# Order of loads, sums and splits around the superblock borders of a three-stage kernel

## The chip, the cores and the metric

The kernel runs as one program on one core of a Trainium2 chip. The metric is the device time of one execution in microseconds; the kernel before takes 1987.39 us (median of 3 runs, 1986.38 to 1988.28).

## The reference

Three stages are chained. A linear attention (4 batches, 8 heads, 576 positions, 64 channels) gives 2304 tokens of 512 channels. A dense two-layer MLP with a leaky ReLU follows. The last stage is a mixture of 8 experts in which every token goes through every expert, weighted by a matrix P that 8 rounds of row and column scaling balance:

```python
P = np.exp(logits - logits.max())          # logits = x @ w_gate, 2304 x 8
for _ in range(8):
    P /= P.sum(1, keepdims=True) + 1e-09
    P /= P.sum(0, keepdims=True) + 1e-09
    P *= N / E
for e in range(E):                          # E = 8, w1 512 x 1024, w2 1024 x 512
    h = np.maximum(x @ w1[e], 0.0)
    out += P[:, e:e + 1] * (h @ w2[e])
```

Everything is float32.

## The kernel before

All matrix products run as three TensorE products of split operands: a value is kept as a rounded high part and a low part, and `split` makes them, the high part by a copy on ScalarE (L526) and the low part by a subtraction on VectorE (L527). The expert stage also uses a scheme with seven block products in place of eight, so sums and differences of the blocks of x, w1, w2 and the hidden values are needed first; their names are A11, S1 to S4 and so on for weights and B11, B21, B22, T1 to T4 for the data side.

The expert stage covers the tokens in 3 superblocks of 768 tokens (two blocks of 384). The first layer of all experts is cut into NQ = 32 pairs of units, so there are NG = 96 groups, `group(i)`: groups 0 to 31 are the first superblock, 32 to 63 the second, 64 to 95 the third. Group i makes the seven first-layer products of its pair. In the first superblock the second layer is done plainly (`y_tile`), while the split operands of both layers are made from the raw weights and written out to HBM (`keep_w1`, `keep_w2`, `keep`). From group 34 on the second layer is done by `y_pass` with the seven products too, and all weight operands come back from HBM through a ring of 256 KB chunks (`ring_load`).

A group has seven steps t0 to t6, and the program text is written in that order, one half step at a time. t0 to t3 issue the seven first-layer products, with the copies of their sums (c1 at L977, c2 at L1000 and L1002) and the activations `relu_split` or `relu_p`; t4 to t6 issue second-layer work. Splits whose low part is still to be made are put on a list (`rest`), and the `drain` of a later step issues it. TensorE, ScalarE, GpSimd and SyncE (SP, which issues every DMA) take their instructions in that written order; each engine waits at its next instruction until the operands are there.

What surrounds the borders between superblocks:

- `second_load(i)` (L523) loads the 512 KB of raw w2 of pair i. In an odd group i of the first superblock `second_ops` issues it for pair i-1 at the end of t0 and for pair i at the end of t1; `pair_w2` splits them at t6 of that group and at t0 of the next one.
- In group 31, t0 issues `ring_load(0, 7)`, then `keep_w1(31)`; t1 issues `p_load(1, 0)` (two loads of rows of P, L774). `ring_load(7, 14)` stands in step t4 of group 31, `ring_load(14, 18)` in t0 of group 32, `ring_load(18, 22)` in t2 of group 33. The chunks 0 to 6 are used by group 32, 7 to 13 by group 33, 14 to 27 by group 34.
- `x_ahead` and `x_next` make the sums of x of the next superblock (GpSimd) and their splits into the tiles that the first-layer products read. For the second superblock both start in group 31; for the third, `x_ahead` runs in group 58 and `x_next` in group 63. The sum T4 is made in `x_next`; for the third superblock the low parts of B11 and T2 are made on GpSimd.
- `op_split` splits the hidden values of a pair of groups into the seven operands of `y_pass`, from the raw products in `raw_q(0)` to `raw_q(3)`; `sub_raw` (L797) makes the differences, on VectorE or GpSimd. `ends(i)` is true for group 63; groups 95 (NG-1), 96 and 97 form the end. `y_pass` adds its results by VectorE (L824) or by a copy (L818) and a GpSimd addition (L819).
- `y_out` transposes finished outputs and copies them out of PSUM, by ScalarE (L897) and VectorE (L895) in turn.
- c2 and the sum T4 come from one pool of two buffers (tag "hh"); before, every group takes the next buffer for c2.

Of the kernel before, what the change touches and what calls it, by code (L numbers as in the profile page):

```python
# [22 lines left out]
def kernel(  # L23
# [500 lines left out]

    def split(hi, lo, a, eng=nc.vector):
        nc.scalar.copy(hi, a)  # L526
        return lambda: eng.tensor_tensor(lo, a, r32(hi), op=ALU.subtract)  # L527

# [76 lines left out]
    def x_split(sb, name, a):  # L605
        eng = nc.gpsimd if sb > 1 and name in ("B11", "T2") else nc.vector
        f = split(xt(name)[:, 0], xt(name)[:, 1], a, eng)

        def end():
            f()  # L610
            ready.add(("xt", sb, name))

        return end
# [28 lines left out]
    def x_ahead(sb):  # L642
        b11, b12, b21, b22 = x_quads(sb)
        t1, t2 = (
            raw_q(k) if sb == 1
            else acc[1][:, k * XS // 2 : (k + 1) * XS // 2].rearrange("p (c n) -> p c n", c=KC // 2)
            for k in range(2)
        )
        x_parts[sb] = t1, t2
        nc.gpsimd.tensor_tensor(t1, b12, b11, op=ALU.subtract)  # L650
        nc.gpsimd.tensor_tensor(t2, b22, t1, op=ALU.subtract)
        nc.gpsimd.tensor_tensor(b12, b22, b12, op=ALU.subtract)

    def x_next(sb):
        b11, b12, b21, b22 = x_quads(sb)
        t1, t2 = x_parts[sb]
        yield
        t4 = hp_.tile([P, KC // 2, BLK], F32, tag="hh", name=f"t4_{sb}")
        rest.append(x_split(sb, "B11", b11))
        yield  # L660
        nc.gpsimd.tensor_tensor(t4, b21, t2, op=ALU.subtract)
        if sb > 1:
            rest.append(x_split(sb, "T2", t2))
        yield
        if sb == 1:
            rest.append(x_split(sb, "T2", t2))
        rest.append(x_split(sb, "T1", t1))
        yield
        rest.append(x_split(sb, "B21", b21))
        yield  # L670
        rest.append(x_split(sb, "T3", b12))
        rest.append(x_split(sb, "B22", b22))
        yield
        rest.append(x_split(sb, "T4", t4))

# [203 lines left out]
    def y_out(sb, dt, ya):  # L879

        c11, c22, dd, cc = ya
        nc.vector.tensor_tensor(dd, c22, dd, op=ALU.subtract)
        nc.vector.tensor_tensor(cc, c22, cc, op=ALU.subtract)
        for th, quads in enumerate(((c11, cc), (dd, c22))):
            for t in range(TB):
                tt = th * TB + t
                if tt % 2 == 0:
                    yield PE_NEXT
                pt = (bank if sb == NSB - 1 else side_bank)(f"po{sb}_{dt}_{tt}")[:, : 2 * P]
                for h, a in enumerate(quads):  # L890
                    nc.tensor.transpose(pt[:, h * P : (h + 1) * P], a[:, t * P : (t + 1) * P], ident)
                n = dt * 2 * TB + tt
                o = acc[1][:, n % 6 * 2 * P : (n % 6 + 1) * 2 * P]
                if t % 2:
                    nc.vector.tensor_copy(o, pt)  # L895
                else:
                    nc.scalar.copy(o, pt)  # L897
                tok = 2 * sb * TB + tt
                nc.sync.dma_start(
                    out[tok * P : (tok + 1) * P, :].rearrange("p (h t n) -> p h t n", h=2, t=2)[:, :, dt],  # L900
                    o.rearrange("p (h n) -> p h n", h=2),
                )

    rest, late = [], []

    def ends(i):
        return NQ < i < NG - 1 and i % NQ == NQ - 1

    def group(i):
# [7 lines left out]
        if i < NG:  # L917
            bk = [bank(f"p{n}_{i}")[:, :BLK] for n in "abcd"]
            c2 = hp_.tile([P, 2, BLK], F32, tag="hh", name=f"c2_{i}")
            c1 = hp_.tile([P, BLK], F32, tag="g", name=f"c1_{i}", bufs=1)  # L920
            add = lambda o, x, y: nc.vector.tensor_tensor(o, x, y, op=ALU.add)  # L921
# [17 lines left out]
        def second_ops(t):  # L939
# [11 lines left out]
            if half == 1 and i < NQ:  # L951
                if t < 2:
                    second_load(i - 1 + t)
                if t == 6:
                    rest.append(pair_w2(i - 1))
                    late.append(lambda: keep_w2(i - 1))

        def t0():
            drain((rest, late))
            if i == NQ - 1:  # L960
                ring_load(0, 7)
            if i == NQ:
                ring_load(14, 18)
            if i == NQ + 2:
                ring_load(22, 30)
            if i >= NG:
                y_steps(0)
                if i == NG:
                    rest.append(op_split(LG, "T2", raw_q(0)))
                    rest.append(op_split(LG, "T3", raw_q(1)))  # L970
                return
            if i < NQ:
                keep_w1(i)
# [5 lines left out]
            add(c1, bk[1], c1)  # L979
            second_ops(0)  # L980
            if new and half and i < NG - 1:
                rest.append(op_split(eg, "T1", raw_q(0)))
            if ends(i - 1):
                sub_raw(nc.vector, 2, 0, 2)
                rest.append(op_split(eg - 1, "T3", raw_q(1)))

        def t1():
            drain()
            if i == NQ - 1:
                p_load(1, 0)  # L990
            if new and i % (2 * EG) == 2 and i + 2 < NG:
                n = i // (2 * EG) + 1
                p_load(n // E, n % E)
            if i >= NG:
                y_steps(1)
                if i == NG:
                    rest.append(op_split(LG, "T4", raw_q(2)))
                return
# [7 lines left out]
            if ends(i - 1):  # L1006
                rest.append(op_split(eg - 1, "T4", raw_q(2)))

        def t2():
            drain()  # L1010
            if i == NQ + 1:
                ring_load(18, 22)
            if i >= NG:
                y_steps(2)
                return
            product(bk[0], i, "A12", "B21", False)
# [4 lines left out]
            product(bk[2], i, "S4", "B22", False)  # L1021
            add(c2[:, 0], bk[2], c1)
            if i == NG - 1:
                rest.append(op_split(eg, "T1", raw_q(0)))
# [3 lines left out]
        def t3():  # L1028
# [6 lines left out]
            if new:  # L1035
                relu_p(i, 0, raw_q(2 * half)[:, 1], c1)
                relu_p(i, 1, raw_q(2 * half + 1), c2)
                if half:
                    sub_raw(nc.vector, 0, 3, 0)
                    if not ends(i):  # L1040
                        sub_raw(nc.gpsimd, 1, 3, 1)
# [5 lines left out]
            if i == NQ - 1:  # L1047
                rest.append(lambda: ring_load(7, 14))

        def t4():  # L1050
# [7 lines left out]
            if new:  # L1058
                if half == 0:
                    rest.append(op_split(eg, "B11", raw_q(0)))  # L1060
                else:
                    rest.append(op_split(eg, "B21", raw_q(2)))
                    rest.append(op_split(eg, "B22", raw_q(3)))

        def t5():
# [5 lines left out]
            if new:  # L1071
                if half == 0:
                    sub_raw(nc.gpsimd, 0, 1, 0)
                else:
                    if ends(i):
                        sub_raw(nc.gpsimd, 1, 3, 1)
                    else:
# [119 lines left out]
    T3 = H2 * (NPH - 1)  # L1197
    at(T3 + 8, pair0)

    for n, t in enumerate((18, 19, 20, 21, 22, 23, 27, 28, 29, 30, 35)):  # L1200
# [88 lines left out]
```

## Time and profile before

| | us |
|---|---|
| median of 3 runs | 1987.39 |
| profiled execution | 1986.21 |
| its span, first to last instruction | 1984.4 |
| TensorE busy | 1938.1 (98%) |
| VectorE busy | 1491.1 (75%) |
| ScalarE busy | 805.2 (41%) |
| GpSimd busy | 708.3 (36%) |
| mean granted TensorE clock | 0.991 of full speed |

The median is 1.2 us above the profiled execution. The share of TensorE leaves 46 us of the span in which it is idle, and short stretches in which its granted clock is lower; the table by stretches in the last section shows where some of that lies. In the rows there, "[3.98 <-ACT c L977]" means that the engine was idle for 3.98 us before the row and that line 977 on ScalarE ended the idle time. PE is TensorE, DVE VectorE, ACT ScalarE, POOL GpSimd, SPq the queue of SyncE.

### The profile page before, as it was taken

The numbers are of one execution on the slowest core, as the hardware profiler recorded it, in microseconds if no ns is written. First come the engines' busy times: TensorE is split into PE (matmuls) and PEld (weight loads), VectorE is DVE, ScalarE is ACT, GpSimd is POOL, SyncE is SP. The second block draws the span as 40 slices with busy tenths as digits, with TensorE's granted clock in tenths as the row PEclk, the third lists the DMA queues.
The fourth block names the chain that finished last, engine by engine and source line by source line (L and its number), as shares of the span: only waits on it lengthen the run. The fifth ranks groups of instructions, "written<-read, shape, count | busy, mean of one in ns | idle before, by whom it ended". The sixth has DMA issues, their size and how long they took to land.

```text
span 1984.4 us, 30153 instructions
## 1 busy us (share of the span) xinstructions
PE 1938.1 (98%) x10757; PEld 1864.1 (94%) x10757; DVE 1491.1 (75%) x2214; ACT 805.2 (41%) x1480; POOL 708.3 (36%) x514
## 2 busy tenths in 40 slices
PE   7999999999999999999989999999999999999998
PEld 6999999999898988899879999999999999999997
DVE  7766535354788787887876888887887888888885
ACT  6744323233444444444433333333344433333333
POOL 4124313100133333343412444435553344434433
PEclk8999999999999999999989999999999999999999
DMA  6402111030388988888778888878878788887884
GB/s 249 166 11 75 54 32 54 22 117 1 133 281 291 313 300 301 298 306 310 268 267 305 260 259 264 257 246 273 256 243 251 250 272 261 261 261 263 258 256 134
DMA packets 237075, 430.43 MB, mean 217 GB/s; under 512 B 19952, under 2 KB 38528, under 8 KB 236928
## 3 DMA queue, kind: packets, MB, share of 16 engines
q1 hardware_dynamic: 236928, 428.51, 65.4%
q8 instruction: 87, 1.43, 0.3%
q14 instruction: 60, 0.49, 0.1%
HBM read 306.20 MB, written 122.23 MB: 216 GB/s over the span
## 4 chain that ended last, share of the span: by engine, by line
PE 46%; DMA 9%; DVE 6%; POOL 2%; ACT 2%; issue 1%; SPq 1%; DVEq 0%; POOLq 0%; ACTq 0%
PE e L199 23%; PE pc L199 6%; PE pd L199 6%; PE pa L199 6%; DMA mo_t<-in_w 6%; PE pb L199 3%; DMA d<-wb_t 2%; DMA d<-wa 1%; DVE c L921 1%; DVE wa L527 1%; POOL mo_t L534 1%; DVE mo_t L797 1%; DVE mo_t L783 1%; ACT wa L526 1%; DVE wb_t L527 1%
## 5 line engine op out<-in xcount | busy, mean ns | idle before, releaser
L819 POOL TENSOR_TENSOR acc<-acc,acc 128x384 f32<-128x384 f32 x188 | 277.0, 1473 | 301.7 <-ACT acc L818 292.0
L199 PE MATMUL e<-wb_t,xs 128*128 128x512 f32 x1152 | 270.4, 393 | 0.0
L199 PE MATMUL e<-xs,wb_t 128*128 128x384 f32 x1392 | 262.7, 335 | 5.6 <-DVE acc L824 3.0
L199 PEld LDWEIGHTS e<-wb_t,xs 128*128 128x128 f32 x1152 | 217.1, 189 | 44.3 <-DVE rc L422 0.2
L199 PEld LDWEIGHTS e<-xs,wb_t 128*128 128x128 f32 x1392 | 242.8, 188 | 6.8 <-DVE acc L824 3.7
L199 PE MATMUL e<-wa,wb_t 128*128 128x384 f32 x1296 | 244.3, 336 | 0.4 <-DVE acc L824 0.3
L527 DVE TENSOR_TENSOR wa<-mo_t,wa 128x768 fp32r<-128x768 f32 (+2 forms) x194 | 201.3, 1053 | 36.9 <-ACT wa L526 35.7
L199 PEld LDWEIGHTS e<-wa,wb_t 128*128 128x128 f32 x1296 | 227.5, 189 | 1.0 <-DVE acc L824 0.7
L818 ACT COPY acc<-e 128x384 f32<-128x384 f32 x188 | 90.3, 480 | 292.5 <-PE e L199 277.8
L797 POOL TENSOR_TENSOR mo_t<-mo_t 128x768 f32<-128x768 f32 x64 | 118.4, 1850 | 244.9 <-DVE mo_t L783 218.2
L526 ACT CAST wa<-mo_t 128x768 fp32r<-128x768 f32 (+2 forms) x194 | 157.5, 842 | 58.4 <-DVE mo_t L797 22.5
L217 DVE TENSOR_TENSOR hh<-g,hh 128x384 fp32r<-128x384 f32 x96 | 61.5, 641 | 156.6 <-ACT g L216 156.5
L533 POOL TENSOR_TENSOR mo_t<-mo_t 128x256 f32<-128x256 f32 x32 | 30.1, 940 | 390.1 <-DMA mo_t<-in_w 168.4
L824 DVE TENSOR_TENSOR acc<-e,acc 128x384 f32<-128x384 f32 x242 | 125.1, 548 | 37.8 <-PE e L199 28.9
L527 DVE TENSOR_TENSOR xs<-mo_t,xs 128x768 fp32r<-128x768 f32 x119 | 125.6, 1066 | 37.1 <-ACT xs L526 37.1
L199 PE MATMUL pd<-xs,wb_t 128*128 128x384 f32 x744 | 149.9, 335 | 2.8 <-DVE xs L527 2.8
L199 PE MATMUL pa<-xs,wb_t 128*128 128x384 f32 x744 | 150.2, 336 | 1.0 <-ACT c L977 1.0
L199 PE MATMUL pc<-xs,wb_t 128*128 128x384 f32 x744 | 149.1, 334 | 0.0
L215 ACT ACTIVATE hh<-ph 128x384 fp32r<-128x384 f32 x96 | 47.3, 493 | 242.3 <-PE y L199 227.6
L199 PEld LDWEIGHTS pd<-xs,wb_t 128*128 128x128 f32 x744 | 130.9, 188 | 3.2 <-DVE xs L527 3.1
L199 PEld LDWEIGHTS pa<-xs,wb_t 128*128 128x128 f32 x744 | 131.4, 189 | 1.8 <-ACT c L977 1.7
L783 DVE SCALAR_TENSOR_TENSOR mo_t<-c,mo_t 128x768 f32<-128x768 f32 (+1 forms) x128 | 128.9, 1011 | 3.0
(164 smaller groups left out, 3638.6 us busy)
## 6 DMA issues: line engine op xcount, KB each, us to landing
wb_t<-d SPq DMA_DIRECT2D x882, 256.0 KB, 3.2
d<-wa SPq DMA_DIRECT2D x32, 1792.0 KB, 8.6
d<-wb_t SPq DMA_DIRECT2D x90, 512.0 KB, 4.0
mo_t<-in_w SPq DMA_DIRECT2D x64, 512.0 KB, 9.6
raw<-in_wm SPq DMA_DIRECT2D x32, 512.0 KB, 3.7
d<-wa SPq DMA_DIRECT2D x22, 512.0 KB, 3.2
mo_t<-pd SPq DMA_DIRECT2D x32, 192.0 KB, 8.1
v<-in_vt SPq DMA_DIRECT2D x16, 320.0 KB, 5.9
```

Source lines behind the costliest of these rows:

```text
L199: nc.tensor.matmul(o, a, b, start=start, stop=stop, **more)
L215: nc.scalar.activation(hh[:, 0, :], p, AF.Prelu, alpha=0.01)
L217: nc.vector.tensor_tensor(hh[:, 1, :], g, r32(hh[:, 0, :]), op=ALU.subtract)
L526: nc.scalar.copy(hi, a)
L527: return lambda: eng.tensor_tensor(lo, a, r32(hi), op=ALU.subtract)
L533: nc.gpsimd.tensor_tensor(s[:, 0], a21, a22, op=ALU.add)
L534: nc.gpsimd.tensor_tensor(a21, a11, a21, op=ALU.subtract)
L783: nc.vector.scalar_tensor_tensor(o, p, 0.0, r, op0=ALU.max, op1=ALU.mult)
L797: eng.tensor_tensor(raw_q(o), raw_q(x), raw_q(y), op=ALU.subtract)
L818: nc.scalar.copy(t, bk[b])
L819: nc.gpsimd.tensor_tensor(c22, c22, t, op=ALU.add)
L824: return nc.vector.tensor_tensor(a, bk[b], a, op=ALU.add)
```

## The change

- `second_load(0)` and `second_load(1)` are issued in the last phase of the MLP, 26 half steps after its start. In odd groups from 3 on, `second_load(i-1)` is the first thing in t0, ahead of `keep_w1(i)` and `pair_sums`.
- In group 31 the order on SP becomes: `second_load(30)` in t0; `p_load`, `second_load(31)`, `ring_load(0, 7)` in t1; `keep_w1(31)` in t3. `ring_load(7, 14)` goes to t3 of group 32, and 14 to 21 are loaded together in t2 of group 33.
- `x_ahead` makes all four sums, T4 too, one in each half step; `x_next` only splits, T1 one step later than before, and all low parts are made on VectorE.
- From group 33 on, all groups use one c2 buffer, and T4 has the other.
- For group 63, B21 and B22 are split in t0 and t1 of the next group instead of t4, the difference in `raw_q(2)` moves from t0 to t1 and the split of T4 from t1 to t2 of the next group, and the difference in `raw_q(1)` moves from GpSimd to VectorE.
- At the end: the difference in `raw_q(0)` of group 94 and that in `raw_q(1)` of group 95 move from GpSimd to VectorE (the latter from t3 to t5), that in `raw_q(2)` moves from t5 of group 95 to t2 of group 96, B21 and B22 are split in t1 of group 96 instead of t4 of group 95, T4 in t2.
- `y_out` copies by ScalarE alone.

The diff, cut to its core:

```diff
-        eng = nc.gpsimd if sb > 1 and name in ("B11", "T2") else nc.vector
-        f = split(xt(name)[:, 0], xt(name)[:, 1], a, eng)
+        f = split(xt(name)[:, 0], xt(name)[:, 1], a)
...
+        t4 = hp_.tile([P, KC // 2, BLK], F32, tag="hh", name=f"t4_{sb}")
         nc.gpsimd.tensor_tensor(t1, b12, b11, op=ALU.subtract)
+        yield
         nc.gpsimd.tensor_tensor(t2, b22, t1, op=ALU.subtract)
+        yield
+        nc.gpsimd.tensor_tensor(t4, b21, t2, op=ALU.subtract)
+        yield
         nc.gpsimd.tensor_tensor(b12, b22, b12, op=ALU.subtract)
...
+        for names in ((), ("B11",), (), ("T2",), ("T1", "B21"), ("T3", "B22"), ("T4",)):
+            for n in names:
+                rest.append(x_split(sb, n, x_parts[sb][n]))
+            yield
...
-                if t % 2:
-                    nc.vector.tensor_copy(o, pt)
-                else:
-                    nc.scalar.copy(o, pt)
+                nc.scalar.copy(o, pt)
...
-            c2 = hp_.tile([P, 2, BLK], F32, tag="hh", name=f"c2_{i}")
+            if i <= NQ:
+                c2_t[0] = hp_.tile([P, 2, BLK], F32, tag="hh", name=f"c2_{i}")
+            c2 = c2_t[0]
...
-                if t < 2:
+                if t < 2 and i > 1 and i + t < NQ:
                     second_load(i - 1 + t)
...
             drain((rest, late))
-            if i == NQ - 1:
-                ring_load(0, 7)
-            if i == NQ:
-                ring_load(14, 18)
+            if half:
+                second_ops(0)
...
-            if i < NQ:
+            if i < NQ - 1:
                 keep_w1(i)
...
             if ends(i - 1):
-                sub_raw(nc.vector, 2, 0, 2)
                 rest.append(op_split(eg - 1, "T3", raw_q(1)))
+                rest.append(op_split(eg - 1, "B21", raw_q(2)))
...
             if i == NQ - 1:
                 p_load(1, 0)
+                second_load(i)
+                ring_load(0, 7)
...
                 if i == NG:
-                    rest.append(op_split(LG, "T4", raw_q(2)))
+                    rest.append(op_split(LG, "B21", raw_q(2)))
+                    rest.append(op_split(LG, "B22", raw_q(3)))
...
             if ends(i - 1):
-                rest.append(op_split(eg - 1, "T4", raw_q(2)))
+                sub_raw(nc.vector, 2, 0, 2)
+                rest.append(op_split(eg - 1, "B22", raw_q(3)))
...
             if i == NQ + 1:
-                ring_load(18, 22)
+                ring_load(14, 22)
...
+                if i == NG:
+                    sub_raw(nc.vector, 2, 0, 2)
+                    rest.append(op_split(LG, "T4", raw_q(2)))
...
+            if ends(i - 1):
+                rest.append(op_split(eg - 1, "T4", raw_q(2)))
...
-                    if not ends(i):
+                    if not ends(i) and i < NG - 1:
                         sub_raw(nc.gpsimd, 1, 3, 1)
...
             if i == NQ - 1:
-                rest.append(lambda: ring_load(7, 14))
+                keep_w1(i)
+            if i == NQ:
+                ring_load(7, 14)
...
-                else:
+                elif not ends(i) and i < NG - 1:
                     rest.append(op_split(eg, "B21", raw_q(2)))
                     rest.append(op_split(eg, "B22", raw_q(3)))
...
-                    sub_raw(nc.gpsimd, 0, 1, 0)
+                    sub_raw(nc.gpsimd if i < NG - 2 else nc.vector, 0, 1, 0)
                 else:
-                    if ends(i):
-                        sub_raw(nc.gpsimd, 1, 3, 1)
+                    if ends(i) or i == NG - 1:
+                        sub_raw(nc.vector, 1, 3, 1)
...
+    at(T3 + 26, second_load, 0)
+    at(T3 + 26, second_load, 1)
```

## Rows read from the trace of the kernel before

**Rows 1.** Busy time by stretch: PE, PEld, DVE, ACT, POOL, clock, DMA share, GB/s.
```profile
996.70:1024.60 27.90, 19.32 (x80) 16.93 (x79) 19.37 (x25) 8.37 (x13) 4.61 (x3) 0.76 0.85 306
1024.60:1463.20 438.60, 438.03 (x2515) 436.26 (x2514) 360.57 (x489) 165.26 (x288) 187.80 (x118) 1.00 0.81 260
1463.20:1489.70 26.50, 23.67 (x127) 23.35 (x127) 24.04 (x27) 13.34 (x22) 14.49 (x8) 0.94 0.75 250
1932.30:1984.40 52.10, 42.48 (x235) 40.08 (x234) 32.19 (x47) 15.07 (x29) 18.12 (x14) 0.95 0.46 140
```

**Rows 2.** TensorE in order of time, groups 32 and 33: start, duration, instruction, idle before.
```profile
1005.02 2.29 PE L199 MATMUL pa<-xs,wa 128*128 128x384 f32 x6 [3.98 <-ACT c L977]
1011.90 2.29 PE L199 MATMUL pc<-xs,wa 128*128 128x384 f32 x6 [4.60 <-ACT c L1000]
...
1031.87 8.36 PE L199 MATMUL e<-wb_t,xs 128*128 128x512 f32 x36
```

**Rows 3.** ScalarE in the same stretch: the splits of raw w2 of pairs 30, 31.
```profile
1002.81 1.04 ACT L526 CAST wb_t<-mo_t 128x1024 fp32r<-128x1024 f32 x1 [4.91 <-DMA mo_t<-in_w]
...
1010.43 1.04 ACT L526 CAST wb_t<-mo_t 128x1024 fp32r<-128x1024 f32 x1 [5.46 <-DMA mo_t<-in_w]
```

**Rows 4.** The queue of SyncE in groups 31 and 32: issue start and time.
```profile
987.00 4.53 SPq L706 DMA_DIRECT2D wa<-d  x7
991.57 0.43 SPq L550 DMA_DIRECT2D d<-wa  x1
992.11 0.50 SPq L523 DMA_DIRECT2D mo_t<-in_w  x1
992.65 3.92 SPq L774 DMA_DIRECT2D mo_t<-pd  x2
996.91 1.51 SPq L523 DMA_DIRECT2D mo_t<-in_w  x1
1001.60 7.83 SPq L706 DMA_DIRECT2D wa<-d  x7
```

**Rows 5.** DMA issues: count, KB each, median us to landing; whole span, then 960:1060.
```profile
wb_t<-d SPq DMA_DIRECT2D x882, 256.0 KB, 3.2
...
wa<-d SPq DMA_DIRECT2D x14, 256.0 KB, 5.9
```

**Rows 6.** TensorE in order of time, groups 58, 64 and 65.
```profile
1394.44 1.32 PE L199 MATMUL pa<-xs,wb_t 128*128 128x384 f32 x6 [0.57 <-ACT c L977]
...
1484.06 1.63 PE L199 MATMUL pd<-xs,wb_t 128*128 128x384 f32 x5 [2.83 <-DVE xs L527]
...
1509.91 1.32 PE L199 MATMUL e<-xs,wb_t 128*128 128x384 f32 x6 [2.01 <-DVE acc L895]
```

**Rows 7.** VectorE, then GpSimd, in order of time around the border of groups 63 and 64.
```profile
1478.32 2.61 DVE L797 TENSOR_TENSOR mo_t<-mo_t 128x768 f32<-128x768 f32 x1
...
1483.06 1.81 DVE L527 TENSOR_TENSOR xs<-acc,xs 128x768 fp32r<-128x768 f32 x2
...
1488.40 0.94 DVE L797 TENSOR_TENSOR mo_t<-mo_t 128x768 f32<-128x768 f32 x1
...
1477.94 2.18 POOL L797 TENSOR_TENSOR mo_t<-mo_t 128x768 f32<-128x768 f32 x1
```

**Rows 8.** TensorE in order of time at the end, group 96.
```profile
1950.79 1.34 PE L199 MATMUL e<-xs,wb_t 128*128 128x384 f32 x6 [2.99 <-DVE acc L824]
...
1952.46 6.87 PE L199 MATMUL e<-wa,wb_t 128*128 128x384 f32 x30 [0.33 <-DVE acc L824]
```

**Rows 9.** VectorE in order of time at the end, groups 94 to 96.
```profile
1933.79 0.96 DVE L783 SCALAR_TENSOR_TENSOR mo_t<-c,mo_t 128x768 f32<-128x768 f32 x1
...
1946.84 3.43 DVE L527 TENSOR_TENSOR xs<-mo_t,xs 128x768 fp32r<-128x768 f32 x2
...
1959.83 0.55 DVE L824 TENSOR_TENSOR acc<-e,acc 128x384 f32<-128x384 f32 x1
```

**Rows 10.** ScalarE at the end, group 95: the copy into c2.
```profile
1936.95 0.48 ACT L1000 COPY c<-pc 128x384 f32<-128x384 f32 x1
```

More of the change, by code (lines that the diff above doesn't have):

```diff
@@ L523, in second_load, with split @@
         nc.sync.dma_start(r2(i), w[u : u + 2, :, DM:].rearrange("u p n -> p u n"))
-    def split(hi, lo, a, eng=nc.vector):
+    def split(hi, lo, a):
         nc.scalar.copy(hi, a)
-        return lambda: eng.tensor_tensor(lo, a, r32(hi), op=ALU.subtract)
+        return lambda: nc.vector.tensor_tensor(lo, a, r32(hi), op=ALU.subtract)
     def pair_sums(i):
@@ L648, in x_ahead @@
         )
-        x_parts[sb] = t1, t2
+        t4 = hp_.tile([P, KC // 2, BLK], F32, tag="hh", name=f"t4_{sb}")
+        x_parts[sb] = {"B11": b11, "T2": t2, "T1": t1, "T3": b12, "B21": b21, "B22": b22, "T4": t4}
         nc.gpsimd.tensor_tensor(t1, b12, b11, op=ALU.subtract)
+        yield
         nc.gpsimd.tensor_tensor(t2, b22, t1, op=ALU.subtract)
+        yield
+        nc.gpsimd.tensor_tensor(t4, b21, t2, op=ALU.subtract)
+        yield
         nc.gpsimd.tensor_tensor(b12, b22, b12, op=ALU.subtract)
     def x_next(sb):
[L655 to L674, printed above, removed]
+        for names in ((), ("B11",), (), ("T2",), ("T1", "B21"), ("T3", "B22"), ("T4",)):
+            for n in names:
+                rest.append(x_split(sb, n, x_parts[sb][n]))
+            yield
     LG = NG // 2 - 1
@@ L904 @@
     rest, late = [], []
+    c2_t = [None]
     def ends(i):
@@ L968, in t0 @@
                 if i == NG:
+                    rest.append(op_split(LG, "T3", raw_q(1)))
                     rest.append(op_split(LG, "T2", raw_q(0)))
-                    rest.append(op_split(LG, "T3", raw_q(1)))
                 return
-            if i < NQ:
+            if i < NQ - 1:
                 keep_w1(i)
@@ L979, in t0 @@
             add(c1, bk[1], c1)
-            second_ops(0)
+            if half == 0:
+                second_ops(0)
             if new and half and i < NG - 1:
```

## The prediction
> **What bounds the kernel now.** I read first the busy table by stretches, then TensorE's waits in order of time, then the engine that ended each wait. In the long middle of the expert stage TensorE is busy for 438.03 of 438.60 us at full clock [rows 1]: nothing off TensorE is worth anything there. Its 2515 matmuls give 0.1742 us each, so a product of six takes 1.045 us and a group of 84 takes 14.6 us. What can be won lies in stretches where TensorE stands still or runs at the lower clock: the border of the first and second superblock (996.7 to 1024.6, busy 19.32 of 27.90 us, clock 0.76), the second border (1463.2 to 1489.7, 23.67 of 26.50, clock 0.94) and the end (1932.3 on, clock 0.95) [rows 1]. 0.76 is a mixture of the two levels, 1.2 and 2.4 GHz: six matmuls after the first wait took 2.29 us [rows 2].
>
> First border: TensorE waits 3.98 us for the copy into c1 and 4.60 us for the copy into c2 [rows 2]. Those copies are short; ScalarE takes them in order and stood 4.91 and 5.46 us in front of the splits of raw w2 of pairs 30 and 31, for a DMA [rows 3]. On SP seven ring loads (1792 KB) and `keep_w1` (seven double chunks, 1792 KB) went ahead of the load of pair 30, and the two loads of P also ahead of that of pair 31, issued only at 996.91 [rows 4]. At the stretch's 306 GB/s [rows 1] the 4096 KB up to the end of load 30 take 13.7 us from 987.0, to 1000.7; its reader started at 1002.81. So the loads are late because of their place in the queue.
>
> Second border: TensorE waits 2.83 us for a low part on VectorE, and later 2.01 us for VectorE's copy of an output [rows 6]. VectorE is simply behind: the same 128x768 difference takes 0.94 us with GpSimd idle and 2.61 us beside a GpSimd difference of 2.18 us [rows 7]. The end: 2.99 and 0.33 us for the additions that empty PSUM, behind two splits that took 3.43 us in place of 1.81 [rows 7 to 9], and 30 matmuls in 6.87 us.
>
> **First border, term by term.** What it loses now: 42 products at 0.1742 are 7.3 us, the 36 wide ones 8.36 less the 0.16 by which records overlap, together 15.5; the stretch took 27.9, so 12.4 us.
>
> After the change load 30 is issued where the ring loads stood, 987.0. Then P takes between 1.0 us (two issues at 0.5) and 3.92 [rows 4], then load 31, at 988.5 to 991.4. Ahead of the end of load 31 lie 512+384+512 KB, 4.7 us at 306 GB/s: both have landed by about 992 to 996, before ScalarE comes to them (about 998 and 1001, by its copies before and with T1's copy of 0.9 us added). Both waits of rows 3 go. What becomes late next:
> - Ring loads 0 to 6 are moved past P and load 31, so issued from 989 to 992. With 3.2 to 5.9 us to landing [rows 5] the first is there at 992.2 to 997.8; group 32 wants it at 996.7. Cost 0 to 1.1, I take 0.2.
> - `keep_w1(31)` behind them delays nobody but ring loads 7 to 13, which overwrite what it reads; the old order had those at 1001.6 [rows 4].
> - Ring loads 7 to 13 now stand behind `keep_w2(31)`, which waits for VectorE's low part of pair 31. I put that at 1003 to 1006, the first landing at 1006 to 1013; group 33 wants it at 1012.2. Cost 0 to 2, I take 0.3, as the issue's 0.65 us a chunk (4.53/7) runs faster than TensorE uses them.
> - ScalarE has T1's copy later than before, so c1 and c2 come up to 1 us late; I take 0.4.
> - Ring loads 14 to 21 together in group 33: eight issues of 0.65 us from about 1015, wanted from 1027 on: hidden.
>
> Gain 12.4 - 0.9 = 11.5 (8.3 to 12.4).
>
> The DMA order has a rule in the Trainium skill, "DMA: Bandwidth & Descriptors", section "Queues, rings and completion order": each DMA engine consumes the descriptors of a ring in ring order. It speaks for the raw loads and as much against ring loads 0 to 6, now behind 1408 KB. The late load 30 agrees with it; what it makes of the ring loads is the first bullet, worked out from rows.
>
> **Early raw loads of pairs 0 and 1, and `second_load` ahead of `keep_w1`.** They change what ScalarE waits for in the first superblock. I have no row of a TensorE wait there that they end, and cost them at nothing; if the earlier load should push `keep_w1` back, TensorE doesn't see that, as it is read back 32 groups later.
>
> **Second border.** Now lost: 26.5 less 126 matmuls at 0.1742 (21.95), 4.5 us. VectorE's work ahead of T3's low part changes by: B21 and B22 of group 63 out (1.8), low parts of B11 and T2 in (1.8), the difference beside GpSimd from 2.61 to 0.94 (-1.7). GpSimd's own two splits and T4's sum also leave this stretch; by the 1.67 us that one GpSimd difference costs VectorE [rows 7] these three are worth 0 to 5, I take 2.5. So T3 comes 1.7 to 6.7 us earlier, I take 4.2, against a wait of 2.83: gone, or 1.1 left at the worst. Behind the border group 64 must now make four splits (3.6 us) in the 7.3 us before its `y_pass` uses them: cost 0 to 3, I take 0.5. The output copy by ScalarE (0.3 to 0.5 us, as its other copies) ends the 2.01; I take 1.9 (1.0 to 2.0). Sum 4.5 - 0.5 + 1.9 = 5.9 (1.4 to 6.5).
>
> **Group 58** now makes four sums in place of three on GpSimd. Three made TensorE wait 0.57 us there [rows 6]. One more costs VectorE 1.7 us by rows 7; VectorE is busy 360.57 of 438.60 us [rows 1], so 2.6 us of a group are free to take it up. I take 0.3 (0 to 1.8). The Trainium skill, "SBUF — State Buffer", section "Who interferes with whom", would make it dearer: the engine that comes second to the shared ports is fully blocked for the whole instruction. By that the fourth sum holds VectorE for all of GpSimd's 2.18 us [rows 7], and TensorE for 0.5 more at most: it stays inside the bound.
>
> **End.** Now lost 2.99 + 0.33 and 6.87 - 30 x 0.1742 - 0.16 = 1.5 of lower clock: 4.8 us. With B21 and B22 gone from group 95 and both GpSimd differences made by VectorE at 0.94, the additions that empty PSUM come some 3 us earlier, and the 2.99 goes. But the two splits and a difference (2.8 us) now stand between the passes of group 96, where the addition at 1959.83 [rows 9] already came just in time. I take 1.2 of these 2.8 as a new wait: gain 3.6 (2.0 to 4.8).
>
> **Sum.** 11.5 + 5.9 - 0.3 + 3.6 = 20.7 us. The profiled execution took 1986.21 and should become 1965.5; the median of the runs is 1.2 above it, so 1987.39 - 20.7 = 1966.7. The bounds add up to 9.9 and 23.7, that is 1977.5 and 1963.7; all at an end at once is unlikely, so the forecast's own range is 1963.7 to 1972.
>
> **Rivals.**
> - The waits move. Ring loads 7 to 13 behind the keep of pair 31, the four splits behind the second border and the three pieces in group 96 all hang on VectorE, which has 18% to spare; where it is further behind than I put it, the terms fall to their low ends. For: every wait of rows 6 and 8 is VectorE's or behind it. Against: seven GpSimd pieces that slow it leave. Gain about 12: 1975. Chance 0.13.
> - The raw loads come no sooner, because `second_load(30)`, now first in the queue, waits for readers of its buffer, or the DMA engines (share 0.85) are the limit. Against: at 987.0 SP was past the keeps of the pair before. The first border stays: gain 9.2, 1978.2. Chance 0.07.
> - Slower: the single c2 buffer. ScalarE's copy into c2 must now wait until VectorE's `relu_p` of the group before has read it. The narrowest place has 1936.95 - 1934.75 = 2.2 us left [rows 9, 10], where one group follows the other after 7.3 us; in all others it is 14.6, so 9.5 us. It decides if VectorE falls 9.5 us further behind; above 20.7/62 = 0.33 us a group the kernel is slower than before, and at 0.5 us, 1997. Against: VectorE has 2.6 us a group to catch up. Chance 0.04.
> - The whole gain falls within the measurement because several of these meet: 1985. Chance 0.04.
> - More than the bounds, from waits of the first superblock that I left out: 1961. Chance 0.04.
>
> **How the numbers follow.** The forecast has 0.68. The predicted time is its 1966.7. Leaving out about 0.15, the range reaches to the two partial cases and to the last: 1961 to 1978. About 0.2% (4 us) is what a measurement can tell from no change here. Faster by more: 0.68 + 0.13 + 0.07 + 0.04, less a little for what I don't see, 0.90; within 0.05; slower 0.05.
>
> **What would show it.** Right: the stretch of group 32 takes about 16 to 17 us at a clock of 1.00, ScalarE has no DMA wait ahead of the two raw splits, no wait of more than 1 us for VectorE in groups 64 and 65, and none of 3 us in group 96. A wait of TensorE for "DMA wa<-d" in group 32 or 33 shows the ring loads late; one for VectorE's L527 or L824 in group 64 or 96 shows the deferred splits. The forecast is wrong if the clock still falls at the first border, or if ScalarE's L1000 waits for VectorE's L783 in group after group.

## The result and the profile after

The changed kernel takes 1970.17 us (median of 5 runs, 1969.0 to 1970.39), the kernel before 1988.28 us beside it (5 runs). The ratio is 0.991, with a 95% interval of 0.9895 to 0.9924: 18 us faster, where 20.7 were predicted (1966.7, range 1961 to 1978). The profiled execution of after took 1970.39 us, its span 1968.2.

First the view of [rows 1], for the same stretches: the first border with the group behind it, the middle, the second border, the end.

```profile
997.90:1013.50 15.60, 15.58 (x78) 14.17 (x79) 15.56 (x22) 5.69 (x9) 2.92 (x3) 1.00 1.04 387
1013.50:1030.60 17.10, 15.82 (x79) 13.98 (x78) 13.27 (x19) 5.53 (x9) 3.94 (x2) 1.00 0.90 330
1030.60:1455.60 425.00, 423.44 (x2438) 422.15 (x2438) 350.19 (x473) 159.84 (x280) 187.89 (x118) 1.00 0.82 262
1455.60:1482.10 26.50, 26.50 (x153) 26.30 (x153) 24.92 (x34) 15.11 (x25) 6.31 (x5) 1.00 0.86 279
1920.20:1968.20 48.00, 40.70 (x236) 38.82 (x234) 30.77 (x47) 15.32 (x31) 14.37 (x12) 0.97 0.51 152
```

Group 32, 27.9 us at a clock of 0.76 before, now takes 15.6 us at 1.00. In the stretch at the second border TensorE is busy throughout (a wait of 1.55 us falls behind it); the end is 4 us shorter. In the middle TensorE stands idle for 1.6 us (0.6 before), and in group 33 for 1.3.

Next TensorE in order of time, where it waits, at the first border, in groups 58 to 60, at the second border and at the end (start, duration, instruction, idle before). These answer [rows 2, 6, 8].

```profile
997.92 1.30 PE L199 MATMUL pa<-xs,wa 128*128 128x384 f32 x6 [1.06 <-DMA wa<-d]
...
1019.13 1.15 PE L199 MATMUL pa<-xs,wa 128*128 128x384 f32 x5 [1.27 <-ACT c L963]
...
1385.44 1.33 PE L199 MATMUL pa<-xs,wb_t 128*128 128x384 f32 x6 [0.57 <-ACT c L963]
...
1402.13 1.32 PE L199 MATMUL pc<-xs,wb_t 128*128 128x384 f32 x6 [0.78 <-ACT c L990]
...
1490.87 0.55 PE L879 MATMUL po<-ident,acc 128*128 128x128 f32 x3 [1.55 <-DVE acc L871]
...
1936.25 2.35 PE L199 MATMUL e<-xs,wb_t 128*128 128x384 f32 x12 [0.46 <-DVE acc L812]
...
1945.88 2.34 PE L199 MATMUL e<-wa,wb_t 128*128 128x384 f32 x12 [0.92 <-issue]
```

The waits of 3.98, 4.60, 2.83, 2.01 and 2.99 us are gone, and small ones stand in their places. (L963 and L990 are the copies into c1 and c2, L871 the subtractions of `y_out`, L812 the additions that empty PSUM.)

The queue of SyncE and the splits of raw w2 on ScalarE, groups 31 and 32, answering [rows 3, 4]:

```profile
982.17 0.36 SPq L560 DMA_DIRECT2D d<-wa  x1
...
984.49 0.84 SPq L523 DMA_DIRECT2D mo_t<-in_w  x1
985.38 1.88 SPq L762 DMA_DIRECT2D mo_t<-pd  x2
987.31 0.59 SPq L523 DMA_DIRECT2D mo_t<-in_w  x1
987.99 8.12 SPq L694 DMA_DIRECT2D wa<-d  x7
997.13 0.37 SPq L550 DMA_DIRECT2D d<-wa  x1
...
1007.56 3.19 SPq L694 DMA_DIRECT2D wa<-d  x7
...
996.81 1.04 ACT L526 CAST wb_t<-mo_t 128x1024 fp32r<-128x1024 f32 x1
...
999.64 1.06 ACT L526 CAST wb_t<-mo_t 128x1024 fp32r<-128x1024 f32 x1
```

Both splits now start without a wait for a DMA: the raw loads come in time.

Where the time went is told most plainly by the starts of the 96 groups (first matmul into pa), after against before. The head, up to group 0, took 3.1 us more (503.43 against 500.30); nothing in it explains that, and in the other runs below it varies from 501.4 to 505.1. From there on, the changed kernel gains 19.3 us: 1.7 in many small waits of groups 0 to 30, 10.8 in groups 31 to 33 (60.3 to 49.5), 4.4 in groups 64 to 66 (54.1 to 49.7) and 4.2 from group 95 on (52.1 to 47.9). It loses 1.4 in groups 59 and 60, and 0.4 in group 35; the latter shows in only one other run, the last, and is put down to no part of the change. As the head alone can hide 3 us, single runs are compared below by stretches; the period of a group without a wait is 15.51 us in groups 0 to 33 and 14.56 behind them.

### The profile page after: what moved, and what is told of

Same layout as the page of the kernel before. It is cut to its first block, busy times and chain, and to the rows that moved or that the text cites. A ratio compares the mean times of both kernels' runs of the same rounds, so it can differ in the third digit from the quotient of the medians.

```text
span 1968.2 us, 30157 instructions
## 1 busy us (share of the span) xinstructions
PE 1933.6 (98%) x10757; PEld 1860.9 (95%) x10757; DVE 1484.8 (75%) x2213; ACT 807.1 (41%) x1486; POOL 692.4 (35%) x509
## 4 chain that ended last, share of the span: by engine, by line
PE 58%; DVE 7%; issue 1%; DMA 1%; ACT 1%; SPq 0%; POOL 0%; DVEq 0%; ACTq 0%
PE e L199 30%; PE pc L199 8%; PE pd L199 8%; PE pa L199 8%; PE pb L199 4%; DVE c L909 1%; DVE mo_t L771 1%; DVE wa L527 1%; DVE mo_t L785 1%; DVE xs L527 1%; DMA wb_t<-d 1%; DVE acc L812 0%; DVE acc L745 0%; DMA d<-wa 0%; ACT wa L526 0%
## 5 line engine op out<-in xcount | busy, mean ns | idle before, releaser
L199 PE MATMUL e<-xs,wb_t 128*128 128x384 f32 x1488 | 280.7, 334 | 1.0 <-ACT acc L882 0.6
L199 PEld LDWEIGHTS e<-xs,wb_t 128*128 128x128 f32 x1488 | 259.7, 188 | 1.7 <-ACT acc L882 0.8
L199 PE MATMUL e<-wa,wb_t 128*128 128x384 f32 x1200 | 227.5, 334 | 0.9 <-issue 0.9
L199 PEld LDWEIGHTS e<-wa,wb_t 128*128 128x128 f32 x1200 | 209.6, 188 | 1.2 <-issue 1.2
L785 POOL TENSOR_TENSOR mo_t<-mo_t 128x768 f32<-128x768 f32 x61 | 113.3, 1858 | 230.0 <-DVE mo_t L771 212.6
L526 ACT CAST wa<-mo_t 128x768 fp32r<-128x768 f32 (+2 forms) x186 | 151.5, 842 | 72.0 <-DVE mo_t L785 34.6
L812 DVE TENSOR_TENSOR acc<-e,acc 128x384 f32<-128x384 f32 x242 | 125.1, 548 | 34.0 <-PE e L199 24.6
L199 PEld LDWEIGHTS pc<-xs,wb_t 128*128 128x128 f32 x744 | 130.7, 188 | 1.3 <-ACT c L990 1.3
```

Source lines behind the costliest of these rows:

```text
L199: nc.tensor.matmul(o, a, b, start=start, stop=stop, **more)
L785: eng.tensor_tensor(raw_q(o), raw_q(x), raw_q(y), op=ALU.subtract)
L812: return nc.vector.tensor_tensor(a, bk[b], a, op=ALU.add)
```

## The experiments

**One: the old order of SyncE, in the changed kernel.** Groups 31 to 33 get back their old order of issues; all else stays.

```diff
-            if half:
+            if half and i != NQ - 1:
                 second_ops(0)
+            if i == NQ - 1:
+                ring_load(0, 7)
+            if i == NQ:
+                ring_load(14, 18)
...
-            if i < NQ - 1:
+            if i < NQ:
                 keep_w1(i)
...
                 p_load(1, 0)
-                second_load(i)
-                ring_load(0, 7)
...
-                keep_w1(i)
-            if i == NQ:
-                ring_load(7, 14)
+                rest.append(lambda: ring_load(7, 14))
```

> The changed kernel with the order on SP of groups 31 to 33 put back (ring loads 0 to 6 and the keep of pair 31 ahead of the raw loads of pairs 30 and 31). If the place of the raw loads in the queue makes the stall of the first border, the group 32 takes again about 27.9 us in place of 15.6, ScalarE waits for the DMA ahead of both raw splits, and the run is some 11 us slower than the changed kernel (about 1981). If it was the earlier sums of x or the single c2 buffer that ended the stall, group 32 stays below 17 us and the time below 1973.

1975.78 us against 1988.15 (ratio 0.9937, 0.9922 to 0.9952). Groups 31 to 33 take 55.2 us: the raw loads are late again, but less so than before.

```profile
1004.52 1.31 PE L199 MATMUL pa<-xs,wa 128*128 128x384 f32 x6 [1.41 <-ACT c L967]
1010.55 2.29 PE L199 MATMUL pc<-xs,wa 128*128 128x384 f32 x6 [4.71 <-ACT c L992]
```

So the old order returns only about half of the gain. Something else in the change pays the other half.

**Two: the new order alone, in the kernel before.** The mirror image.

```diff
             if i == NQ - 1:
-                ring_load(0, 7)
-            if i == NQ:
-                ring_load(14, 18)
+                second_ops(0)
...
-            if i < NQ:
+            if i < NQ - 1:
                 keep_w1(i)
...
                 p_load(1, 0)
+                second_load(i)
+                ring_load(0, 7)
...
-                rest.append(lambda: ring_load(7, 14))
+                keep_w1(i)
+            if i == NQ:
+                ring_load(7, 14)
```

> The kernel before with nothing but the new order on SP in groups 31 to 33. By the queue theory groups 31 to 33 together fall from 60.3 to about 49.5 us and the run gains about 11 us (1977). If the gain needs the other parts too (less work for VectorE at the border), a new stall of several us for VectorE shows in group 32 and the gain is below 6.

1980.07 us (ratio 0.9964, 0.9951 to 0.9976), groups 31 to 33 53.2 us: the order alone is worth 7.1 us of 60.3. What is left are waits for an operand and for the ring loads, which start late because the whole queue does:

```profile
984.19 0.97 PE L199 MATMUL pb<-xs,wa 128*128 128x384 f32 x4 [1.50 <-DVE wa L527]
...
1001.68 2.03 PE L199 MATMUL pa<-xs,wa 128*128 128x384 f32 x6 [3.10 <-DMA wa<-d]
```

Where the queue starts late is seen at the keep that opens it in group 31 (`d<-wa`, S4's). It waits for VectorE's low part of wa. VectorE and GpSimd in order of time there, in the kernel before:

```profile
980.17 4.48 DVE L527 TENSOR_TENSOR wa<-mo_t,wa 128x768 fp32r<-128x768 f32 x2
...
979.73 1.86 POOL L651 TENSOR_TENSOR mo_t<-acc,mo_t 128x768 f32<-128x768 f32 x1 [1.70 <-DVE wa L527]
981.55 2.55 POOL L652 TENSOR_TENSOR acc<-acc 128x768 f32<-128x768 f32 x1
```

and in the changed kernel:

```profile
979.30 2.85 DVE L527 TENSOR_TENSOR wa<-mo_t,wa 128x768 fp32r<-128x768 f32 x2
...
987.63 2.19 DVE L909 TENSOR_TENSOR c<-c 128x384 f32<-128x384 f32 x1
...
978.86 1.87 POOL L652 TENSOR_TENSOR mo_t<-acc,mo_t 128x768 f32<-128x768 f32 x1 [1.69 <-DVE wa L527]
985.05 1.84 POOL L654 TENSOR_TENSOR t<-acc,mo_t 128x768 f32<-128x768 f32 x1 [4.32 <-DVE xs L752]
986.85 2.56 POOL L656 TENSOR_TENSOR acc<-acc 128x768 f32<-128x768 f32 x1
```

Before, GpSimd went from T2's sum straight on to b12's, and VectorE's two low parts beside it took 4.48 us. Now T4's sum comes between; it waits 4.32 us for its buffer, b12's sum falls some 4 us later against the group, and the low parts take 2.85. Its price moved to the c addition at 987.63 (2.19 us, 0.55 otherwise), for which TensorE does not wait. That was a reading of two traces; the next run tests it.

**Three: GpSimd's old order alone**, at the first border of the changed kernel.

```diff
         nc.gpsimd.tensor_tensor(t2, b22, t1, op=ALU.subtract)
         yield
+        if sb == 1:
+            nc.gpsimd.tensor_tensor(b12, b22, b12, op=ALU.subtract)
         nc.gpsimd.tensor_tensor(t4, b21, t2, op=ALU.subtract)
         yield
-        nc.gpsimd.tensor_tensor(b12, b22, b12, op=ALU.subtract)
+        if sb > 1:
+            nc.gpsimd.tensor_tensor(b12, b22, b12, op=ALU.subtract)
```

> The changed kernel with one part undone at the first border only: GpSimd makes the sum b12 directly behind T2's and ahead of T4's, as it did before. The theory after the first runs: half of the gain of groups 31 to 33 came from this order, because b12's sum beside VectorE's low part of wa slowed that part, so that the keep from wa reached SyncE 2.5 to 4 us later and the whole queue behind it. Expected then: VectorE's low part takes 4 us or more in place of 2.85, the keep starts 3 us or more behind the start of group 31 (1.0 in the changed kernel), groups 31 to 33 take about 53 us in place of 49.5. Rival: the earlier second_load or T1's place gave that half, and groups 31 to 33 stay within 0.7 us of 49.5.

Groups 31 to 33 take 51.2 us. In the changed kernel and the five runs below that leave this border alone (the ones on the sums of groups 58 to 61, the copies, GpSimd's low parts, the old place of the splits, and the end) they take 48.1 to 49.5, mean 48.7. So in this one run the order costs 2.5 us, 1.7 against the highest of them: the direction is right, the size short of the 3.5 that I expected. VectorE's two low parts and the keep on SyncE, in this kernel:

```profile
978.41 4.50 DVE L527 TENSOR_TENSOR wa<-mo_t,wa 128x768 fp32r<-128x768 f32 x2
...
982.94 0.36 SPq L560 DMA_DIRECT2D d<-wa  x1
...
998.49 1.28 PE L199 MATMUL pa<-xs,wa 128*128 128x384 f32 x6 [2.51 <-DMA wa<-d]
```

The low parts are slowed as before (4.50), the keep starts 2.6 us behind group 31 (980.32), and TensorE waits 2.51 us for the first ring load. But in the kernel before, the keep stood 4.9 us behind the group (984.67 against 979.79), in the changed kernel 1.0 (982.17 against 981.20). Of the 3.9 us the order of the sums thus explains 1.6. The other 2.3 lie further back: VectorE's low parts start 1.9 us ahead of group 31 here and in after, and 0.4 behind it in before. In before VectorE is late from its low part of the raw w2 of pair 28 on. That waits for ScalarE's copy, and the copy for the raw load, which stands behind `keep_w1(29)` (L550) in the queue. These are the lines of before, then of after:

```profile
953.47 0.65 SPq L550 DMA_DIRECT2D d<-wa  x1
954.21 2.70 SPq L523 DMA_DIRECT2D mo_t<-in_w  x2
...
963.93 1.05 ACT L526 CAST wb_t<-mo_t 128x1024 fp32r<-128x1024 f32 x1 [3.47 <-DMA mo_t<-in_w]
...
965.01 1.23 DVE L527 TENSOR_TENSOR wb_t<-mo_t,wb_t 128x1024 fp32r<-128x1024 f32 x1 [2.50 <-ACT wb_t L526]
```

```profile
953.01 0.50 SPq L523 DMA_DIRECT2D mo_t<-in_w  x1
953.55 1.23 SPq L550 DMA_DIRECT2D d<-wa  x1
...
960.38 1.04 ACT L526 CAST wb_t<-mo_t 128x1024 fp32r<-128x1024 f32 x1
...
962.44 1.22 DVE L527 TENSOR_TENSOR wb_t<-mo_t,wb_t 128x1024 fp32r<-128x1024 f32 x1
```

ScalarE's copy starts 15.9 us ahead of group 31 in before and 20.8 ahead in after. From 965.01 on, VectorE in before stands still for only 1.8 us until the low parts of wa begin, so the lateness stays. All three kernels with before's first superblock have this wait of ScalarE (3.5 to 4.5 us); all with the changed one, the first experiment too, have none there. In before it comes 13 times in the first superblock, 2.8 to 4.3 us each, once for each odd group from 5 to 29; in after a single one of 1.6 us is left. So the two early raw loads, and `second_load` ahead of `keep_w1` in the odd groups, move the first superblock's chain of loads, splits and low parts some 2.3 us forward against TensorE. That is read from the traces; no run undid it by itself. That the wait came back with every odd group speaks for the order there, but which of the two does it stays open.

**Four: the loads of P behind ring loads 0 to 6.**

```diff
-                p_load(1, 0)
                 second_load(i)
                 ring_load(0, 7)
+                p_load(1, 0)
```

> The changed kernel with the two loads of P behind ring loads 0 to 6 instead of ahead of them. While they ran, the DMA engines moved only 36 to 67 GB/s for some 5 us, so if these loads hold the queue up, the wait of 1.06 us for the ring load at the start of group 32 is gone and the ring loads land in about 3 to 6 us. If only the bytes ahead count, taking 384 of 1408 KB away leaves 0.7 us or more of the wait.

1966.11 us. The wait for "DMA wa<-d" is gone, group 31 takes 15.51 us; in the changed kernel and the five runs that leave this border alone it takes 15.75 to 17.03. So being moved past P costs 0.2 to 1.5 us, about 1. The page of transfers of the changed kernel, 980 to 1000, shows what P does to those behind it (busy tenths and GB/s in slices of 0.5 us):

```profile
DMA  0000009999999999996121111234436999999999
GB/s 0 0 0 0 0 0 344 385 352 389 373 381 369 315 176 213 385 401 216 36 67 50 47 48 46 66 106 133 151 114 253 406 401 414 406 406 406 385 393 406
```

For some 3.5 us from 989.5 on the engines move 36 to 67 GB/s, and under 160 for two more, though the ring loads are queued; the median one of these takes 7.3 us to land. In the run with P behind them the fall comes after the ring loads: 54 to 134 GB/s for 1.5 us from 993.5 on.

**Five: another place for S4's operand of the last pair**, so that its split needn't wait for the keep of S1.

```diff
-        st = stage(4 * g + k)
+        st = stage(4 * g + k) if 4 * g + k < 2 * NQ - 1 else later["wb"][:, 10 * OW : 12 * OW]
```

> The changed kernel with the last split of the second layer (S4 of pairs 30, 31) staged in chunks 10 and 11 of the other weight buffer, so that it need not wait until the keep of S1 has been written out. If that keep, late on SP, holds ScalarE and through it TensorE in group 33, the 1.27 us wait there goes and group 33 takes 15.5 to 15.9 us in place of 17.15. If the single c2 buffer or VectorE holds ScalarE, group 33 stays at 17.

1967.48 us; group 33 takes 15.51 us (15.78 to 17.15 in the six runs, mean 16.7), so 0.3 to 1.6 gained. In the changed kernel the wait of 1.27 for c1 came from this line of ScalarE:

```profile
1018.08 0.62 ACT L526 CAST wa<-mo_t 128x512 fp32r<-128x512 f32 x1 [5.53 <-DMA d<-wa]
```

The copy into c1 stood behind a split that waited 5.53 us for a keep, and that keep stood behind ring loads 7 to 13 and a store of outputs in the queue.

**Six: the sums one in each group**, groups 58 to 61, in place of one in each half step.

```diff
+        gap = 7 if sb > 1 else 1
         nc.gpsimd.tensor_tensor(t1, b12, b11, op=ALU.subtract)
-        yield
+        for _ in range(gap):
+            yield
...
```

> The changed kernel with the four sums of x for the third superblock one a group (groups 58 to 61) in place of four in a row in group 58. If GpSimd's four pieces in a row put VectorE behind and make the waits of groups 58 to 60, the three groups take 43.7 us in place of 45.9. If the single c2 buffer makes group 59 long, it stays at 15.6.

1968.07 us. Groups 58 to 60 take 45.4 us in place of 45.9 (43.7 without waits): the spread gains 0.5 us, not the 2.2 expected. Group 59 is back at 14.56 us, without a wait, but groups 58 and 60 take 15.42 each. This is group 60:

```profile
1413.87 1.32 PE L199 MATMUL pa<-xs,wb_t 128*128 128x384 f32 x6 [0.56 <-ACT c L967]
```

So the loss of group 59 was that of the sums in a row, not of the single c2 buffer, which all these groups share. A sum still costs something in an even group, where it takes 2.56 us, and nothing in an odd one, where it takes 1.85.

**Seven and eight: the copies of `y_out`**, shared with VectorE again in the changed kernel, then all given to ScalarE in the kernel before.

```diff
-                nc.scalar.copy(o, pt)
+                if t % 2:
+                    nc.vector.tensor_copy(o, pt)
+                else:
+                    nc.scalar.copy(o, pt)
```

> The changed kernel with the output copies of y_out by ScalarE and VectorE in turn, as before. If the copies by VectorE were the reason of the 2.01 us wait of the kernel before, groups 65 and 66 lose about 2 us more than the 35.0 us of the changed kernel. If the wait only moved to the subtractions ahead of the transposes, because VectorE is behind, they stay within 0.6 us of 35.0.

> The kernel before with one part of the change alone: the copies of y_out all by ScalarE. In the changed kernel undoing this part cost groups 64 to 66 3.5 us. If it is worth as much by itself, these groups take 50.6 us in place of 54.1; by the prediction's term of 1.9 they take 52.2; if it is worth nothing until the relief of VectorE is there too, they stay at 54.1.

In the changed kernel groups 65 and 66 go from 35.0 to 38.6 us: the copies by ScalarE are worth 3.5 there. In the kernel before they are worth 1.7 (groups 64 to 66: 54.1 to 52.4), near the 1.9 of the prediction. The difference is this line of the seventh run, which answers the last of [rows 6]:

```profile
1496.17 3.92 PE L199 MATMUL e<-xs,wb_t 128*128 128x384 f32 x12 [2.25 <-DVE acc L883]
```

The wait for VectorE's copy is 2.25 us, and the matmuls behind it run at a granted clock of 0.57 (12 in 3.92 us; 12 take 2.34 us behind the wait of 0.92 at the end). In before the granted clock behind the wait of 2.01 us was 1.00.

**Nine and ten: the rest of the second border.** Low parts of B11 and T2 back on GpSimd; B21, B22 and T4 of group 63 split where they were before.

```diff
+        eng = nc.gpsimd if sb > 1 and name in ("B11", "T2") else nc.vector
```

> The changed kernel with the low parts of B11 and T2 for the third superblock back on GpSimd. If GpSimd's pieces beside VectorE are a main cause of the 4.5 us at the second border, group 64 loses 1 us or more of its 14.7 us back; by the rival, that deferring the splits of pair 63 alone gave it, group 64 stays below 15.0.

```diff
             if ends(i - 1):
+                sub_raw(nc.vector, 2, 0, 2)
                 rest.append(op_split(eg - 1, "T3", raw_q(1)))
-                rest.append(op_split(eg - 1, "B21", raw_q(2)))
...
-                elif not ends(i) and i < NG - 1:
+                elif i < NG - 1:
                     rest.append(op_split(eg, "B21", raw_q(2)))
                     rest.append(op_split(eg, "B22", raw_q(3)))
```

> The changed kernel with B21 and B22 of groups 62 and 63 split ahead of the border again (t4 of group 63), and the difference and T4 one step earlier, as before. If their two splits of 0.9 us ahead of T3's low part decide, TensorE waits 1 to 3 us at S3 x T3 in group 64 again; by the rival, that taking work off GpSimd alone gave it, group 64 stays below 15.0.

Both come out level: groups 64 to 66 take 50.0 us in either, 49.7 in the changed kernel. With the splits in their old place group 64 pays 1.8 more and group 65 1.6 less:

```profile
1474.25 1.31 PE L199 MATMUL pc<-xs,wb_t 128*128 128x384 f32 x6 [0.80 <-ACT c L990]
...
1476.14 1.15 PE L199 MATMUL pd<-xs,wb_t 128*128 128x384 f32 x5 [0.40 <-DVE xs L527]
```

The deferral hence takes the wait out of group 64 and hands it to the subtractions L871 in group 65. Neither part by itself explains why the 2.83 us of [rows 6] went. The two undone together, and the other pieces (the sums made ahead, the difference moved to VectorE) undone alone, weren't tried.

**Eleven: the old end**, the part for the last pair undone.

```diff
-                elif not ends(i) and i < NG - 1:
+                elif not ends(i):
                     rest.append(op_split(eg, "B21", raw_q(2)))
                     rest.append(op_split(eg, "B22", raw_q(3)))
...
-                    sub_raw(nc.gpsimd if i < NG - 2 else nc.vector, 0, 1, 0)
+                    sub_raw(nc.gpsimd, 0, 1, 0)
...
-                    if ends(i) or i == NG - 1:
+                    if ends(i):
                         sub_raw(nc.vector, 1, 3, 1)
```

> The changed kernel with one part undone: the last pair's operand splits behind the border (the part for i from 94 on) stand as they did before. If this part gave the end its gain, the stretch from the start of group 95 to the end of the span goes back from 47.9 us to about 52.1 us, the wait at the last border shows again at about 3 us on an eviction of y, and the time is about 4.2 us above the changed kernel's, near 1974 us. Rival: the end gained from the copies or from the raw loads, and the stretch stays at about 48 us.

From group 95 to the end of the span 52.0 us in place of 47.9, and the wait of [rows 8] is back. The time, 1971.71, is less far above that of after than this, because groups 0 to 35 were 2.4 us shorter in this run. The wait:

```profile
1936.44 1.32 PE L199 MATMUL e<-xs,wb_t 128*128 128x384 f32 x6 [2.98 <-DVE acc L812]
```

**Twelve: what the runs point to**, put together: P behind ring loads 0 to 6 and S4's other place (the edits of the fourth and fifth experiments), one sum in each of the odd groups 55, 57, 59 and 61, and the second half of `y_out`'s subtraction ahead of the first.

```diff
+        gap = 14 if sb > 1 else 1
...
+        nc.vector.tensor_tensor(cc, c22, cc, op=ALU.subtract)
         nc.vector.tensor_tensor(dd, c22, dd, op=ALU.subtract)
-        nc.vector.tensor_tensor(cc, c22, cc, op=ALU.subtract)
...
-        if i == 2 * NQ - 6:
+        if i == 2 * NQ - 9:
```

> The changed kernel with four further moves: the broadcast loads of P behind the first seven ring loads (its one look gained 1.5 us in groups 31 to 33), the last pair's fourth operand staged earlier (1.6 in group 33 and 0.4 in group 35), two sums made ahead in every odd group from 55 to 61 in place of all eight in a row (the spread of one a group gained 1.2 in groups 58 to 60; 0.8 more if the waits in the even groups go), and the second half of y_out's subtraction ahead of the first (0 to 0.5). If the gains add, the median is 5 to 6 us below the changed kernel's 1970.2, at about 1964.5 us. If they replace one another as the parts at the second border did, it is 2 to 3 us, at about 1967.5.

(The text speaks of two sums a group and eight in a row; it is one a group, four in all. And the spread had gained 0.5, not 1.2.) The sums in the changed kernel, and the second and third of them here, on GpSimd:

```profile
1380.77 2.56 POOL L650 TENSOR_TENSOR acc<-acc,acc 128x768 f32<-128x768 f32 x1
1383.41 2.44 POOL L652 TENSOR_TENSOR acc<-acc,acc 128x768 f32<-128x768 f32 x1
1385.92 2.44 POOL L654 TENSOR_TENSOR t<-acc,acc 128x768 f32<-128x768 f32 x1
1388.33 2.56 POOL L656 TENSOR_TENSOR acc<-acc 128x768 f32<-128x768 f32 x1
```

```profile
1362.67 1.85 POOL L654 TENSOR_TENSOR acc<-acc,acc 128x768 f32<-128x768 f32 x1
...
1391.79 1.84 POOL L657 TENSOR_TENSOR t<-acc,acc 128x768 f32<-128x768 f32 x1
```

Two groups apart and in the odd ones, a sum takes 1.85 us in place of 2.44 to 2.56: it no longer runs against VectorE's work.

1962.99 us (median of 4, 1960.99 to 1965.88) against 1987.66: ratio 0.9877, 0.9861 to 0.9894, where the changed kernel had 0.991. Groups 31 to 33 take 46.5 us, three periods without a wait, groups 58 to 60 43.7, also none, and groups 64 to 66 49.3. Against the changed kernel's profiled run these are 2.9 (2.2 against the mean of 48.7), 2.2 and 0.5 us; 1.5 more come from a shorter head. The gains of separate places added.

```profile
979.90:1026.40 46.50, 46.50 (x235) 42.18 (x234) 45.37 (x59) 19.78 (x31) 11.22 (x6) 1.00 0.90 314
```

## Why the prediction was right, and where its steps were not

**First border, size right, cause half wrong.** The term was 11.5; measured 10.8 in the profiled run, and 11.5 if the mean of the six runs (48.7) is set against before's 60.2 (60.3 and 60.2 in two traces). But I put all of it down to SyncE's order in groups 31 to 33. That order alone gives 7.1 when added to before, and its undoing costs after 6.5 (55.2 less 48.7). The failed steps are two that I costed at nothing. GpSimd's sums at this border, which I looked at only for group 58, give 2.5. "Early raw loads of pairs 0 and 1, and `second_load` ahead of `keep_w1`", for which I had "no row of a TensorE wait", move the queue some 2.3 us forward; the 2 us or so that are left of the 11.5 fit that, but were not undone alone. I had looked for waits of TensorE that end in superblock 1, not for how far its chain of loads stands ahead when the border comes; ScalarE's 13 waits for raw w2 were the rows that showed it. By my own price (load 30 at 987.0) the queue would have started as late as in the second experiment, and so with 53 us instead of 49.

**The small terms of that border.** Ring loads 0 to 6: 0.2 taken, bound 1.1, measured 1.06 in the profile and about 1 in the fourth experiment. I had the landing time from [rows 5], but not that it grows to 7.3 us behind P. Ring loads 7 to 13: late for nobody as loads (the row shows no such wait), but I left out what stands behind them, the keep of S1, which the split of S4 waits for: 1.27 at TensorE, within the bound of 2 that I gave for another reason, so here the size came out by luck. T1's copy on ScalarE: 0.4 taken; no wait of TensorE shows it.

**Second border, right but dearer.** 5.9 taken, 4.4 measured, inside 1.4 to 6.5. The 2.83 us went, though no single part could be shown to do it. The four deferred splits, taken at 0.5, cost 1.6 in group 65 (17.7 us against 16.1 in the run with the old place) and leave a wait of 1.55 for L871, where I had said that none over 1 us for VectorE would stand. The copies were sized right as a change of before (1.7 against 1.9), and are worth more in the changed kernel: 3.5.

**Group 58 and after.** 0.3 taken, bound 1.8, measured 1.4, in groups 59 and 60. My reason for the small value, VectorE's 2.6 us of free time per group, was wrong: a group's free time didn't take up what the sums held back. Four of them one behind the other leave waits in three groups; one in each group gains 0.5 back, and one in each odd group costs nothing, as the last experiment shows. The dearer price that the Trainium skill gave ("SBUF — State Buffer", "Who interferes with whom": the second engine at the shared ports is blocked for the whole instruction) had stayed inside the bound. The trace agrees in kind: one c addition on VectorE, begun inside a GpSimd sum of 2.56 us, takes 2.19 us and ends 0.4 behind it; otherwise it takes 0.55.

**End.** 3.6 taken, 4.2 measured, and 4.1 in the run that undid it. The 1.2 for new waits in group 96 was about right: 0.46 and 0.92 show, 1.4 together (the profile names no releaser for the second). Too small was the loss of before, 4.8: its 54 matmuls from 1946.60 to 1961.81 took 15.2 us and are 9.4 at 0.1742, so 5.8 were lost there.

**The rivals.** Waits moved, but small ones: 1.3 in group 33, 1.4 in 59 and 60, 1.6 in 65, 4.3 us together, not that rival's 8 (1975 less 1966.7). The raw loads did come sooner. The single c2 buffer costs nothing that a row shows: groups between the borders keep 14.56 us. The waits of the first superblock that I left out exist (1.7 us), and the head's 3 us, which I had not seen as a spread, took them back in the profiled run.

So of the 20.7, 19.3 us were there from group 0 on, and the medians differ by 18.1. The prediction was right through its sum; the attribution inside its largest term was not. That this term came out so well is in part luck: the cause it names gives 7.1 of its 11.5, and two causes priced at nothing give the rest.

## What to carry to other kernels

When a border of two stages waits for a late load, look at two things: the order in the queue, and how late the queue itself starts; the keep or load that opens it has a chain of its own behind it, over several engines. A part that one run shows to be worth x in the old kernel may be worth another amount in the new one, so test a change from both sides: add a part alone, and take it alone away. Work on GpSimd is placed, not only counted: the same sum lengthens a low part that opens the queue by 1.6 us at one place, and at another a c addition that TensorE doesn't wait for.

## What had not been expected of the hardware

Two loads of P, 384 KB together, let the transfers fall from 350 to 400 GB/s to 36 to 67 GB/s for 3.5 us, and ring loads queued behind them landed in 7.3 us. In the kernel with P behind the ring loads these landed in 6.4 us and TensorE did not wait. And the part of the kernel ahead of the expert stage differs by up to 3.7 us between the profiled runs of kernels in which this part is the same (501.4 to 505.1), more than most of the single terms here.
